# Attention and two feed-forward layers on one core: in batch 0, the value product with unscaled probabilities as stationary operand

## The chip, the cores and the metric

One core of one Trainium2 chip runs the whole program. The metric is the device time of one execution in microseconds. A profiled execution of the same kernel gives the trace from which the rows below come.

## The reference

Causal attention by blocks of 64 over 4 batches, 8 heads, 576 tokens, head size 64; its output, with the heads side by side, is a matrix x of 2304 tokens by 512. Two feed-forward layers follow, each 512 to 2048 to 512, with different nonlinearities. All data is float32.

```python
scores = scale * np.matmul(q, k.transpose(0, 1, 3, 2))
mask = block_i >= block_j                       # blocks of 64 tokens
scores = np.where(mask, scores, -1000000000.0)
scores = scores - np.max(scores, axis=-1, keepdims=True)
attn = np.exp(scores)
attn = attn / (np.sum(attn, axis=-1, keepdims=True) + 1e-09)
attn_out = np.matmul(attn, v)
x = attn_out.transpose(0, 2, 1, 3).reshape(B * S, H * D)
h = x @ w_in;   x = np.maximum(0.01 * h, h) @ w_out            # layer 1
h = x @ w_in2;  g = np.where(h >= 1, h, np.where(h <= -1, 0, (h + 1) ** 2 / 4));  out = g @ w_out2
```

## The kernel before, in words

The kernel keeps float32 accuracy. Most products are made from operands split into a high and a low part of a faster format (three products each, `three`). Only batch 0's attention uses plain float32 products, which the engine runs as two passes, each with its own weight load; `plain_s` and `plain_v` say so for scores and values (`PF` and `VF` are 8 for batch 0, 0 for the others).

A head's 576 tokens are five query tiles (64, then four of 128), in two groups: tiles 0 to 2 (320 tokens) and tiles 3 and 4 (256 tokens). Key chunk 0 has 64 keys, the others 128. For each tile, `scores` (L261) multiplies q by k into a bank of the tag "att" (five banks), VectorE takes the maximum (L286), ScalarE the exponential (L300) and with it the row's sum (the read of the accumulator, same line); VectorE then adds a small constant to the sum and takes the reciprocal (L306 or L308, L309), and GpSimd multiplies the probabilities by it (L47 through `scale`, by `norm_0`). `transposes` (L360) turns each tile by TensorE (L374, two banks of the tag "y"), and ScalarE copies it into the tiles `pT0h` and `pT1h`, keys on partitions. `values` (L403) multiplies, for each group and key chunk, the values as stationary operand (128 columns, of which the first 64 are this chunk's) with all of the group's probabilities as moving operand (128 to 320 columns, L424), into the one bank of the tag "h"; ScalarE copies the first 64 rows of the result into x, which has features on partitions (L432).

While this runs, the weights of layer 1 are loaded and converted: `to_float32` (L104) puts two words together on VectorE (L113 to L115) and scales one on ScalarE or GpSimd by turns (`fE_e`), `split_w` makes high and low parts. After batch 0's attention the blocks of 256 tokens go through layer 1: `split_x` splits x, `up1` (L537 to L539) and `down1` (L567 to L570) multiply, and the attention of batches 1 to 3 is spread between them. `up1` takes the same single "h" bank. Layer 2 comes last.

The program's text is not the order on the engines: `arrange` (L817) runs a model of the engines over all that was traced up to the end of the attention. Each engine takes the ready instruction that stands earliest in the program, with times from `span` (L764), and the order that comes out is written into the program as a chain on each engine, the DMA queue of SyncE included.

## Time and profile before

| | us |
|---|---|
| median of 3 runs | 1029.13 (1028.93 to 1029.42) |
| the profiled execution | 1026.92 |
| its span, first to last instruction | 1025.1 |
| TensorE busy in it | 995.7 (97%) |
| VectorE, ScalarE, GpSimd busy | 709.0, 473.1, 195.8 |

Busy times are sums over the span. An instruction counts as busy from its start to its end, and consecutive ones overlap, so a high share alone does not show that an engine is the one that the others wait for.

### The profile page before, as it was taken

To read this page: it belongs to the slowest core of one execution; us is meant where nothing else is said; L and a number is where in the kernel's file an instruction comes from. 1 tells how busy PE (TensorE), PEld (TensorE's weight loads), DVE (VectorE), ACT (ScalarE), POOL (GpSimd) and SP (SyncE) were. 2 spreads that over 40 slices of the span, in tenths; PEclk is the share of its full clock that TensorE was granted. 3 is DMA by queue.
4 is the path that set the end of the run, shared out by engine and by line. 5 is a ranking of instruction groups with operands and counts; after the bars stand their busy time and mean duration, and the time that the engine had idled before them with its cause. 6 is when DMAs were issued, how large, how long until landed. Compare 5 with 4: busy or idle time off the path is not lost. (4 is left out here: it accounts for less than half of the span.)

```text
span 1025.1 us, 16641 instructions
## 1 busy us (share of the span) xinstructions
PE 995.7 (97%) x5518; PEld 844.8 (82%) x5518; DVE 709.0 (69%) x1859; ACT 473.1 (46%) x1174; POOL 195.8 (19%) x275
## 2 busy tenths in 40 slices
PE   9999999999999999899999999999999999999998
PEld 6668878878878888798989898888888888888897
DVE  7999999997888977887787887334334433443344
ACT  6887767764655545454444443223222222322233
POOL 4452033342242654543010100000000000000000
PEclk9999999999999999999999999999999999999999
DMA  8546232237677766665899784001000100000010
GB/s 320 189 161 224 84 87 61 71 74 160 142 158 154 170 148 145 144 144 107 295 290 297 232 287 104 1 1 61 22 1 1 62 1 1 31 11 0 1 42 20
DMA packets 194117, 115.39 MB, mean 113 GB/s; under 512 B 148208, under 2 KB 167152, under 8 KB 194032
## 3 DMA queue, kind: packets, MB, share of 16 engines
q1 hardware_dynamic: 165840, 106.47, 37.9%
q10 hardware_dynamic: 28192, 7.87, 3.2%
q8 instruction: 43, 0.70, 0.3%
q14 instruction: 42, 0.34, 0.1%
HBM read 83.62 MB, written 30.67 MB: 111 GB/s over the span
## 5 line engine op out<-in xcount | busy, mean ns | idle before, releaser
L537 PE MATMUL h<-xh,w1i 128*128 128x256 f32 x576 | 166.4, 289 | 7.1 <-ACT g L542 6.9
L538 PE MATMUL h<-xl,w1i 128*128 128x256 f32 x576 | 163.7, 285 | 1.0 <-DVE xl L38 0.9
L539 PE MATMUL h<-xh,w1i 128*128 128x256 f32 x576 | 163.4, 284 | 0.0
L719 ACT ACTIVATE sq<-cl,half 128x512 f32<-128x512 f32 (+1 forms) x80 | 54.4, 680 | 200.1 <-DVE cl L718 195.8
L718 DVE TENSOR_SCALAR cl<-hh 128x512 f32<-128x512 f32 (+1 forms) x80 | 51.0, 637 | 111.5 <-PE hh L539 111.3
L537 PEld LDWEIGHTS h<-xh,w1i 128*128 128x128 f32 x576 | 109.1, 189 | 16.8 <-ACT g L542 12.0
L300 ACT ACTIVATE p<-s,nm 64x64 f32<-64x64 f32 (+2 forms) x192 | 91.1, 478 | 63.8 <-DVE nm L286 29.9
L537 PE MATMUL hh<-yh,w2i 128*128 128x512 f32 (+1 forms) x320 | 118.1, 369 | 0.0
L538 PE MATMUL hh<-yl,w2i 128*128 128x512 f32 (+1 forms) x320 | 118.0, 369 | 0.0
L567 PE MATMUL y<-w1o,gh 128*128 128x512 f32 x288 | 117.3, 407 | 0.7 <-DVE yx L575 0.5
L539 PE MATMUL hh<-yh,w2i 128*128 128x512 f32 (+1 forms) x320 | 117.9, 368 | 0.0
L568 PE MATMUL y<-w1o,gh 128*128 128x512 f32 x288 | 114.5, 398 | 0.0
L735 PE MATMUL o<-w2o,ggh 128*128 128x512 f32 x288 | 114.0, 396 | 0.0
L734 PE MATMUL o<-w2o,ggl 128*128 128x512 f32 x288 | 114.0, 396 | 0.0
L538 PEld LDWEIGHTS h<-xl,w1i 128*128 128x128 f32 x576 | 109.0, 189 | 5.5 <-DVE xl L38 1.9
L539 PEld LDWEIGHTS h<-xh,w1i 128*128 128x128 f32 x576 | 109.0, 189 | 0.9
L570 PE MATMUL y<-w1o,gl 128*128 128x512 f32 x288 | 92.4, 399 | 2.7 <-DVE gl L38 2.6
L286 DVE TENSOR_REDUCE nm<-s 128x1 f32<-128x288 f32 (+2 forms) x192 | 80.0, 424 | 8.2 <-PE s L277 4.5
L733 PE MATMUL o<-w2o,ggh 128*128 128x512 f32 x288 | 84.1, 396 | 0.0
L720 DVE TENSOR_TENSOR gg<-hh,sq 128x512 f32<-128x512 f32 (+1 forms) x80 | 50.9, 637 | 47.1 <-ACT sq L719 46.9
L722 DVE TENSOR_TENSOR ggl<-gg,ggh 128x512 fp32r<-128x512 f32 (+1 forms) x80 | 51.1, 638 | 46.7 <-ACT ggh L721 46.2
L542 ACT ACTIVATE g<-h 128x256 f32<-128x256 f32 x144 | 54.2, 378 | 57.5 <-PE h L539 43.1
(111 smaller groups left out, 2038.5 us busy)
## 6 DMA issues: line engine op xcount, KB each, us to landing
wr<-in_w_dram SPq DMA_DIRECT2D x64, 512.0 KB, 5.2
wdram<-wt SPq DMA_DIRECT2D x32, 256.0 KB, 3.9
w<-wdram SPq DMA_DIRECT2D x16, 512.0 KB, 5.6
rq<-in_qkv_dram SPq DMA_DIRECT2D x24, 288.0 KB, 3.0
rk<-in_qkv_dram SPq DMA_DIRECT2D x24, 288.0 KB, 2.9
pT1l<-z SPq DMA_DIRECT2D x16, 384.0 KB, 3.8
ydram<-yx SPq DMA_DIRECT2D x72, 64.0 KB, 2.3
out_dram<-osb ACTq DMA_DIRECT2D x18, 256.0 KB, 3.6
```

The source lines that it names most:

```text
L286: mark["D"] = nc.vector.tensor_reduce(nm[:n, j:j + 1], s[:n, :kw], axis=AX.X, op=ALU.max, negate=True)
L300: mark["A"] = nc.scalar.activation(o, s, AF.Exp, bias=nm[:n, 0:1], scale=es, accum_out=sm[:n, j:j + 1])
L537: nc.tensor.matmul(ps_ap, wh, xh, start=first, stop=False)
L538: nc.tensor.matmul(ps_ap, wh, xl, start=False, stop=False)
L539: nc.tensor.matmul(ps_ap, wl, xh, start=False, stop=last)
L567: nc.tensor.matmul(yt[m], gh[:, ms], wh, start=f == 0, stop=False)
L568: nc.tensor.matmul(yt[m], gh[:, ms], wl, start=False, stop=False)
L570: nc.tensor.matmul(yt[m], gl[:, ms], wh, start=False, stop=f == KF - 1)
L719: nc.scalar.activation(sq[:, :n], cl[:, :n], AF.Square, bias=half[:, 0:1], scale=0.5)
L733: nc.tensor.matmul(ot[m], gh[:, ms], wh, start=f == 0, stop=False)
L734: nc.tensor.matmul(ot[m], gl[:, ms], wh, start=False, stop=False)
L735: nc.tensor.matmul(ot[m], gh[:, ms], wl, start=False, stop=f == KF - 1)
```

## The change

In batch 0 the exponentials are no longer divided by their sum before the transposes. The value product is turned round: for each query tile and key chunk the tile's 128 columns of (unscaled) probabilities are stationary, and the chunk's 64 values with a column of ones are the moving operand (65 columns), so that the result has tokens on partitions and the sum in column 64. One bank holds all five tiles of a head. After the second group VectorE adds the constant to the five sums, takes their reciprocals, and multiplies the 320 results by them into a tile `xt` that a pair of heads shares (it takes the buffers of `pT0l` and `pT1l` by turns). After the odd head TensorE transposes the five tiles of `xt` into two "y" banks, and ScalarE copies these into x. The sum on ScalarE (`accum_out`) goes. The value load writes pieces of 64 elements with gaps between, and the memset of the column of ones is on GpSimd. The conversion's scale is on ScalarE alone (`fE_e`). A branch for unscaled q is added and switched off (`qU` is 'n'). The planner's `span` gets other times for plain float32 products and reciprocals. Batches 1 to 3 keep their code.

```diff
-C = {..., 'fE_e': 'AP', ...}
+C = {'qU': 'n', 'qlE': 'D', ..., 'fE_e': 'A', ..., 'xeE_0': 'A'}
...
         if plain_v(i):
-            nc.sync.dma_start(f32(vv).rearrange("p k a d -> p (k a d)")[:, :vn * D], qkv[row, :, QKC:QKC + vn * D])
-            nc.vector.memset(f32(vv).rearrange("p k a d -> p (k a d)")[:, vn * D:(vn + 1) * D], 0.0)
+            nc.sync.dma_start(f32(vv)[:, :vn, 0], qkv[row, :, QKC:QKC + vn * D].rearrange("p (k d) -> p k d", d=D))
+            nc.gpsimd.memset(f32(vv)[:, :vn, 1, 0:1], 1.0)
...
             mark["A"] = nc.scalar.activation(
-                o, s, AF.Exp, bias=nm[:n, 0:1], scale=es, accum_out=sm[:n, j:j + 1]
+                o, s, AF.Exp, bias=nm[:n, 0:1], scale=es, accum_out=None if plain_v(i) else sm[:n, j:j + 1]
             )
         yield
+        if plain_v(i):
+            return
...
+        if plain_v(i):
+            if g == 0:
+                av[i] = psum(tag, f"v{i}")
+            a = av[i][:, :NKT * (D + 1)].rearrange("p (t d) -> p t d", d=D + 1)
+            hi = ptT(i, g)[0]
+            for t in ts:
+                for c in range(t + 1):
+                    k = 64 if c == 0 else P
+                    q = col(g, c, TILES[t][0] - g0)
+                    nc.tensor.matmul(
+                        a[:, t], hi[:k, q:q + P], f32(vv)[:k, c].rearrange("p a d -> p (a d)")[:, :D + 1],
+                        start=c == 0, stop=c == t,
+                    )
+            yield
+            if g == 1:
+                rc = st_p.tile([P, NKT], F32, tag="rv", name=f"rv{i}", bufs=2)
+                nc.vector.tensor_scalar(rc, a[:, :, D], EPS, None, op0=ALU.add)
+                nc.vector.reciprocal(rc, rc)
+                if h % 2 == 0:
+                    z = h // 2 % 2
+                    xt[b, h // 2] = f32(p_p.tile([P, DW[z]], F32R, tag=f"pT{z}l", name=f"xt{b}_{h // 2}"))[:, :NKT * P].rearrange("p (t c) -> p t c", c=P)
+                x = xt[b, h // 2]
+                d = x[:, :, h % 2 * D:h % 2 * D + D]
+                nc.vector.tensor_tensor(d, a[:, :, :D], rc.unsqueeze(2).to_broadcast([P, NKT, D]), op=ALU.mult)
+                if h % 2 == 1:
+                    yield
+                    for u in range(len(GROUPS)):
+                        u0, un, uts = GROUPS[u]
+                        e = psum(C["T0"], f"xT{i}_{u}")
+                        for t in uts:
+                            q0, n = TILES[t]
+                            nc.tensor.transpose(e[:, q0 - u0:q0 - u0 + n], x[:n, t], ident[:n, :n])
+                        copy(nc, pick("xeE", u, phase(i)), x32[b][:, h // 2, u0:u0 + un], e[:, :un])
+            return
...
-            if plain_v(i):
-                k = 64 if c == 0 else P
-                vr = f32(vv).rearrange("p k a d -> p (k a d)")[:k, c * D:(c + 2) * D]
-                nc.tensor.matmul(a[:, first:gn], vr, ptT(i, g)[0][:k, cs], start=c == 0, stop=c == last)
-                continue
...
-        if plain_v(i):
-            copy(nc, pick("xeE", g, phase(i)), xo, a[:D, :gn])
...
         if srcs[0][3] == F32 and not ins.is_transpose:
-            return w / 0.6 + 165, w / 0.6 + 95, 0
+            step = 2 * max(w / 1.2 + 3, 108) * (1.33 if srcs[1][2][0][1] == 64 and w > 64 else 1)
+            return step + 120, step, 0
...
         if op == "Reciprocal":
-            return 150, 72, 0
+            return 149 + w / 0.96, 71 + w / 0.96, 0
```

## Rows read from the trace of the kernel before

**Rows 1.** Batch 0's stretch: start:end, length, busy PE, PEld, DVE, ACT, POOL; clock; DMA.
```profile
4.60:84.00 79.40, 74.92 (x365) 51.96 (x365) 76.21 (x301) 63.82 (x200) 40.48 (x54) 0.98 0.64 219
```
**Rows 2.** Waits of TensorE, 4 to 85 us: total us, times, longest.
```profile
PE t L374 <- ACT pT1h L30: 2.0, 2, 1.5
PE s L277 <- ACT p L300: 1.6, 2, 1.2
PE t L374 <- issue: 0.7, 1, 0.7
...
```
**Rows 3.** Waits of TensorE, 85 to 200 us.
```profile
PE v L427 <- DVE pT1l L38: 1.1, 1, 1.1
...
```
**Rows 4.** Timeline of the weight loads, 43.5 to 47.9 us: start, us, what, rows*columns.
```profile
44.59 0.19 PEld L277 LDWEIGHTS s<-kh,qs 128*64 128x64 f32 x2 [0.38 <-DVE rc L309]
44.86 0.29 PEld L424 LDWEIGHTS v<-pT1h,vv 64*128 64x128 f32 x2
45.48 1.59 PEld L424 LDWEIGHTS v<-pT1h,vv 128*128 128x128 f32 x8 [0.33 <-issue]
46.99 0.80 PEld L374 LDWEIGHTS t<-ident,p 128*128 128x128 f32 x7
...
```
**Rows 5.** Weight loads by form, 0 to 83 us: busy us, mean ns | idle before.
```profile
L424 PEld LDWEIGHTS v<-pT0h,vv 64*128 64x128 f32 x16 | 2.4, 185 | 3.3 <-ACT pT1h L30 1.3 <-issue 0.9 <-ACT w1o L30 0.7
L277 PEld LDWEIGHTS s<-kh,qs 128*64 128x64 f32 x16 | 1.6, 144 | 1.7 <-issue 0.8 <-DVE rc L309 0.4 <-DVE rc L306 0.2
...
```
**Rows 6.** Timeline of the matmuls around two value products.
```profile
44.86 2.41 PE L424 MATMUL v<-pT1h,vv 64*128 64x256 f32 x10
47.10 0.93 PE L374 MATMUL t<-ident,p 128*128 128x128 f32 x7
...
75.64 1.65 PE L424 MATMUL v<-pT0h,vv 64*128 64x320 f32 x6
77.13 0.71 PE L374 MATMUL t<-ident,p 128*128 128x128 f32 x5
```
**Rows 7.** VectorE's groups of instructions, 0 to 83 us.
```profile
L113 DVE TENSOR_SCALAR wr<-wr 128x512 int32<-128x512 uint32 x16 | 8.1, 508 | 0.0
L309 DVE RECIPROCAL rc<-rc 128x1 f32<-128x1 f32 (+1 forms) x44 | 6.4, 149 | 0.1
L308 DVE TENSOR_SCALAR rc<-sm 128x1 f32<-128x1 f32 (+1 forms) x36 | 4.8, 138 | 0.2 <-ACT p L300 0.2
L38 DVE TENSOR_TENSOR xl<-x,xh 128x256 fp32r<-128x256 f32 x1 | 0.4, 403 | 0.0
...
```
**Rows 8.** The conversion step on VectorE, 83 to 200 us.
```profile
L113 DVE TENSOR_SCALAR wr<-wr 128x512 int32<-128x512 uint32 x16 | 6.5, 431 | 0.0
...
```
**Rows 9.** GpSimd's groups, 0 to 83 us.
```profile
L47 POOL TENSOR_SCALAR p<-p,rc 64x64 f32<-64x64 f32 (+4 forms) x40 | 28.8, 725 | 34.5 <-DVE rc L309 9.7 <-DVE rc L308 8.6 <-ACT pT0h L30 3.3
...
```
**Rows 10.** ScalarE's groups, 0 to 83 us.
```profile
L300 ACT ACTIVATION_READ_ACCUMULATOR p<-s,nm 128x1 f32 (+1 forms) x52 | 10.3, 198 | 0.0
L43 ACT ACTIVATE w<-wr 128x512 f32<-128x512 f32 x10 | 6.7, 674 | 0.0
L30 ACT ACTIVATE x<-v 64x320 f32<-64x320 f32 (+1 forms) x15 | 6.0, 402 | 0.4 <-PE v L424 0.2
...
```
**Rows 11.** Timeline of the end of batch 0's attention, some instructions.
```profile
79.70 3.39 PE L424 MATMUL v<-pT1h,vv 64*128 64x256 f32 x10
80.67 0.72 POOL L38 TENSOR_TENSOR xl<-x,xh 128x256 fp32r<-128x256 f32 x1 [1.18 <-ACT xh L30]
83.13 0.38 ACT L30 ACTIVATE x<-v 64x256 f32<-64x256 f32 x1 [2.02 <-PE v L424]
84.04 0.48 PE L537 MATMUL h<-xh,w1i 128*128 128x256 f32 x1
...
```
**Rows 12.** Two stretches there; columns as in rows 1, the clock after POOL's.
```profile
77.50:80.90 3.40, 1.88 (x12) 1.27 (x10) 3.36 (x15) 3.32 (x10) 1.11 (x2) 1.00 0.22 80
80.90:84.30 3.40, 3.40 (x15) 3.03 (x14) 3.12 (x9) 1.33 (x5) 1.52 (x3) 0.50 0.71 223
...
```

More of the change, by code (lines that the diff above doesn't have):

```diff
@@ L212, in attention_moe_moe @@
     stk = {}
+    av, xt = {}, {}
     def plain_s(i):
@@ L217, in plain_s, with unscaled @@
         return p < len(C["PF"]) and h < C["PF"][p]
+    def unscaled(i):
+        return pick("qU", 0, phase(i)) == "y"
     def plain_v(i):
@@ L241, in load_head @@
             nc.sync.dma_start(r, qkv[row, :, q0:q1])
-            scale(nc, pick("qhE", 0, ph), qs[:, q0:q1], r, SCALE)
-            nc.vector.scalar_tensor_tensor(
-                out=qs[D:, q0:q1], in0=r[D:], scalar=SCALE, in1=f32(qs)[D:, q0:q1], op0=ALU.mult, op1=ALU.subtract
-            )
+            if unscaled(i):
+                copy(nc, pick("qhE", 0, ph), qs[:, q0:q1], r)
+                tt(nc, pick("qlE", 0, ph), qs[D:, q0:q1], r[D:], f32(qs)[D:, q0:q1], ALU.subtract)
+            else:
+                scale(nc, pick("qhE", 0, ph), qs[:, q0:q1], r, SCALE)
+                nc.vector.scalar_tensor_tensor(
+                    out=qs[D:, q0:q1], in0=r[D:], scalar=SCALE, in1=f32(qs)[D:, q0:q1], op0=ALU.mult, op1=ALU.subtract
+                )
             r = raw_p.tile([P, S], F32, tag="raw", name=f"rk{i}")[:, :kn]
@@ L268, in scores @@
         nm = st_p.tile([P, 2], F32, tag="nm", name=f"nm{i}_{t}")
-        sm = st_p.tile([P, 2], F32, tag="sm", name=f"sm{i}_{t}")
-        rc = st_p.tile([P, 1], F32, tag="rc", name=f"rc{i}_{t}")
+        if not plain_v(i):
+            sm = st_p.tile([P, 2], F32, tag="sm", name=f"sm{i}_{t}")
+            rc = st_p.tile([P, 1], F32, tag="rc", name=f"rc{i}_{t}")
         sc = []
@@ L292, in scores @@
             sc.append((p[:n].rearrange("p (a k) -> p a k", a=2), halves))
-        es = SCALE / 2 if plain_s(i) else 1.0
+        es = SCALE / 2 if plain_s(i) else SCALE if unscaled(i) else 1.0
         if np_ > 1:
@@ L407, in values @@
         g0, gn, ts = GROUPS[g]
+        if h == 0 and g == 0:
+            x32[b] = one_p.tile([P, KC, S], F32, tag="x", name=f"x{b}", bufs=2)
+        if plain_v(i):
[10 more added lines that the diff above has]
+                        start=c == 0, stop=c == t,
+                    )
+            yield
[19 more added lines that the diff above has]
+            return
         a = psum(tag, f"v{i}_{g}")
         last = ts[-1]
-        if h == 0 and g == 0:
-            x32[b] = one_p.tile([P, KC, S], F32, tag="x", name=f"x{b}", bufs=2)
         own, other = (0, D) if h % 2 == 0 else (D, 0)
@@ L430, in values @@
                 )
[L431 to L440 removed]
+        tmp = two_p.tile([P, 320], F32, tag="sc", name=f"tmp{i}_{g}", bufs=C["sc"])
+        nc.scalar.activation(tmp[own:own + D, :gn], a[other:other + D, :gn], AF.Copy)
+        if pick("fold", 0, phase(i)) == "D":
+            nc.vector.tensor_tensor(xo, a[own:own + D, :gn], tmp[own:own + D, :gn], op=ALU.add)
+        else:
+            nc.scalar.activation(xo, a[own:own + D, :gn], AF.Copy)
+            nc.gpsimd.tensor_tensor(xo, xo, tmp[own:own + D, :gn], op=ALU.add)
         yield
```

9 lines of the change are left out of this document (1 added, 8 removed).

## The prediction

> **What bounds the kernel now.** I read the busy time by stretch first. While batch 0's attention runs, up to the first matrix product of the feed-forward part at 84 us, TensorE is busy 74.92 of 79.40 us and VectorE 76.21 [rows 1]. Both look full, so the question is which one makes the other wait. TensorE's own list of waits settles it: between 4 and 85 us it stands still for 4.5 us in all (four rows, the three longest shown), and 1.5 of these are one wait, at 79.6 us [rows 2]. From 85 to 200 us its waits come to 2.9 us (five rows, the first shown) [rows 3]. VectorE fills its gaps with the conversion of weights that the next stage wants. So TensorE paces batch 0 and most of what follows: what the change adds on TensorE is paid nearly in full, and what it takes from the other engines brings back at most those waits.
>
> A busy TensorE also has gaps inside. The weight loads of the value product show them: two loads of 64 rows go back to back (0.29 us for two), then the loads of 128 rows start only after 0.33 us of idle [rows 4]. The first stream starts when the first load is done, at 44.97 us; two streams of 256 columns at 0.213 us end at 45.39, and the next load starts at 45.48, so 0.09 us after the stream. With equal rows the loads hide behind streams: eight loads take 1.59 us, one per stream. I count a change of rows (64 to 128 or back) as 0.09 us of idle plus a load of 0.107 us that is not hidden.
>
> **The change part by part: TensorE.** Before, a head's value product runs from 44.86 to 47.10 us for the second group (2.24 us) and from 75.64 to 77.13 for the first (1.49) [rows 6]; with 0.09 us ahead of each for the change into 64 rows that is 3.91 us, with 4 changes of rows in it.
>
> After, a head has 15 products (1+2+3+4+5 key chunks), each in two passes as now: 30 passes. The stationary operand is the 128 columns of probabilities and only 65 columns stream (0.054 us), so the load sets the pace. Two loads of this width take 0.29 us together and one alone 0.185, so they follow each other by some 0.107; and that a load hides behind a stream as short as this is seen at 44.59 us, where two loads of 64 columns take 0.19 us together and one alone 0.144, the second one starting 0.05 us after the first, as the first stream starts [rows 4, 5]. With the start of the stream I count 0.108 us a pass. 30 x 0.108 = 3.24 us. Key chunk 0 has 64 rows and now comes once per query tile, not once per group: going into it and out of it makes 8 changes of rows per head (tiles 0 and 1 share one stretch) in place of 4. At a change, one pass costs 0.054 + 0.09 + 0.107 = 0.25 us, 0.145 more than 0.108: 8 x 0.145 = 1.16. The load behind each group is half uncovered, 0.05 us twice. Sum 4.50 us against 3.91: +0.59 per head, +4.7 us for eight.
>
> New are the transposes of x, five per pair of heads: 5 x 0.11 (seven transposes' loads take 0.80 us [rows 4]) and the 64-token tile's two changes of rows, 2 x 0.15, makes 0.85 us, or 3.4 us for four pairs. TensorE gets 4.7 + 3.4 = 8.1 us more work. Bounds: if the added changes of rows cost nothing, 4 x 0.145 x 8 = 4.6 us go, and 3.5 are left; if nothing hides behind 65 columns, each pass costs 0.161 (30 x 0.161 + 8 x 0.09 = 5.55 per head) and the sum is over 16 us. The pair of 64-column loads speaks against that end, so I take 8.1, and for the range the case that no wait is recovered.
>
> A rule of the Trainium skill (TensorE: Matmul & The Clock Gate, section "Part 3: Packing small matmuls", on what overlaps) says that weight loads overlap a running matmul only where their row group differs. The rows above show the reverse here: equal rows overlap, a change of rows leaves 0.33 us. By the rule the added changes would be free, and TensorE's part of the sum about 3.5 us.
>
> **The other engines.** VectorE loses 40 additions (0.138 us) and 40 reciprocals (0.149 us) [rows 7], 11.5 us busy, though consecutive small ones overlap by about half, so 8 us; eight memsets go to GpSimd. It gains per head an addition, a reciprocal and a product of 320 elements: 0.14 + 0.15 + 0.50 (0.403 for 256 elements [rows 7], in proportion) = 0.79, or 6 us. GpSimd loses the 40 normalisations, 28.8 us [rows 9]; one of the steps that convert weights on VectorE takes 0.508 us in this stage, with them about [rows 7]; a later one without such company, 0.431 [rows 8], so 16 x 0.08 = 1.2 us come back there, perhaps twice that with the other steps. In all VectorE gets 3 to 5 us lighter. ScalarE loses 48 accumulator reads (0.198) and 16 copies of x (0.402), gains 8 wider copies of about the same length and six conversions (0.674) from GpSimd [rows 10]: 9.5 + 6.4 - 3.2 - 4.0, so 9 us lighter. None of this is on the path; its worth is that TensorE's transposes no longer wait for sum, reciprocal and normalisation, which is part of the 4.5 us in [rows 2]. Without the wait at the end of the stage 3.0 us are to be had; ScalarE's copies and the score banks still stand behind some of it, so I take 2.5, between 0 and 3.0. In the following stage conversion is further ahead; of the 2.9 us I take 1.5, between 0 and 2.9. The value load now lands in five pieces of 256 B per partition; it is issued a head ahead, and I cost it at nothing, as its cover is a whole head (some 9 us). The disabled branch (unscaled q) and the planner's new estimates do no work on the chip; the latter give other orders, for which I allow 1.5 us either way.
>
> **The handover.** Now the last head's second group ends, ScalarE copies x out of the one "h" bank (at 83.13 us), and the feed-forward starts at 84.04 [rows 11]. After, the bank is free only when VectorE's three operations are done, and the last quarter of x goes through them (0.79), transposes (0.9), a copy (0.4), the split on ScalarE and GpSimd (0.4 + 0.72 [rows 11]): with hand-offs about 4 us, of which three quarters of the first product (9 of 12 passes, 84.04 to 85.1) and batch 1's scores and transposes cover most. The batch 1 tiles pT0l and pT1l now wait for the transposes of x, which takes away some of that cover. Against this the present stall of 1.5 us [rows 2] and the half clock behind it should go or be replaced by the same. Net +0.5 us, between -2.5 and +2.
>
> Sum: 8.1 - 2.5 - 1.5 + 0.5 = +4.6 us on the profiled execution's 1026.92, so 1031.5; the median of the runs shown is 2.2 us above that execution, which gives **1033.7 us**.
>
> **The rivals.** First, no change: the weight loads of 64 and of 128 rows overlap in the new order, so the added changes of rows cost nothing, TensorE's addition is 3.5 us, and the recovered waits pay for it: 3.5 - 2.5 - 1.5 + 0.5 = 0, 1029.1 us. For it: the planner may put chunk 0 of neighbouring tiles next to the 64-token transposes. Against: the change of rows in [rows 4] has its idle. The rule of the skill named above would have it so. Chance 0.17.
>
> Second, faster: VectorE paces the stage after all; its 76.21 of 79.40 us [rows 1] leaves no room, and what is taken from it, up to 5 us, carries through to the end of conversion. TensorE's 8.1 us then fall into gaps between its instructions that the list of waits does not show, and 4.5 us remain as gain: 1024.6 us. It decides if those gaps are over 8 us in the stage; against it, all waits listed come to 4.5 us [rows 2]. Chance 0.17.
>
> Third, slower by more: the clock. It was at half in one stretch, 80.9 to 84.3 us, right after TensorE was busy only 1.88 of 3.40 us [rows 12]; there ten value passes took 3.39 us against 2.41 [rows 6, 11], so a fall costs 1 to 1.7 us. The changed kernel streams 30 x 0.054 = 1.6 us per head in the value product, where now 2 x 1856 columns (320 + 128 + 128 and five times 256) stream for 3.1. If gaps there bring three more falls, +4.2 us: 1038 us. Chance 0.16.
>
> **How the numbers follow.** The forecast has 0.50, with 1030.5 to 1037.5 as its own range. A measurement of this kernel tells about 0.2% (2 us) from no change. Faster: 0.17 from the second rival and 0.02 from the first; same: 0.13 from the first and 0.05 from the forecast; the rest is slower, 0.63. The range leaves out most of the second rival and reaches over the third: 1026.5 to 1039.5, which takes in the case in which no wait comes back (8.1 + 2, 1039.2).
>
> **What would show it.** Right: the first feed-forward product starts 4 to 7 us later than 84.04; the loads of the new value product have a pace near 0.108 us with idle "issue" of about 0.2 us before each change of rows; GpSimd nearly empty; TensorE's waits in this stage no more than before. Wrong: loads of 64 and 128 rows without idle between them, a first product at or before 84 us, VectorE no longer full, or several stretches at half clock before 85 us.

## The result and the profile after

The changed kernel takes 1040.1 us (median of 4 runs, 1038.4 to 1045.2) against 1029.0 for the kernel before in the same series: 1.0121 times as long, interval 1.0101 to 1.014. It is slower, as forecast, but by 11.1 us where 4.6 were forecast, and above the upper end of the range. The profiled execution is one of the four, 1040.94 us with a span of 1039.2: 14.0 us above the profiled execution of before. Some 3 of these 14 us belong to the two executions and not to the kernels: the one profiled after lies 0.8 us above its kernel's median, the one before 2.1 below.

The page's first part for the changed kernel (busy us, share of the span, number of instructions):

```profile
PE 1006.9 (97%) x5650; PEld 861.5 (83%) x5650; DVE 709.6 (68%) x1795; ACT 470.9 (45%) x1124; POOL 161.8 (16%) x237
```

TensorE has 11.2 us more, GpSimd 34 us less, and VectorE is where it was over the whole span. Where the 14 us arose is read from three points of TensorE's timeline: the last matmul of batch 0's value products, the first matmul for the fourth column of 128 hidden features in the first block's `up1`, and the last matmul of all (the start of each). I call the stretch up to the first point the body and that between the first and the second the end; three columns of `up1` lie in it.

| us | body ends | end ends | length of the end | rest, to the last matmul |
|---|---|---|---|---|
| before | 82.7 | 92.1 | 9.4 | 928.8 |
| after | 86.7 | 106.1 | 19.4 | 928.9 |
| difference | +4.0 | | +10.0 | +0.1 |

The forecast had +5.6 for the body (8.1 of work less 2.5 of waits), +0.5 for the end and -1.5 for the rest.

The view of stretches, of the changed kernel: start:end, length, busy time of PE, PEld, DVE, ACT and POOL, granted clock, DMA share, GB/s. The first row is the body, the second the end, the other four show how the end goes:

```profile
4.60:86.70 82.10, 80.92 (x487) 63.33 (x486) 73.15 (x236) 61.92 (x150) 4.90 (x12) 0.98 0.66 217
86.70:106.10 19.40, 14.69 (x72) 12.96 (x71) 16.05 (x43) 11.27 (x28) 5.17 (x4) 0.74 0.63 220
86.70:89.30 2.60, 0.71 (x9) 0.57 (x7) 2.54 (x11) 1.56 (x3) 1.85 (x2) 0.98 0.47 134
89.30:92.70 3.40, 3.40 (x15) 3.06 (x16) 3.31 (x10) 1.76 (x7) 0.00 (x0) 0.52 0.82 227
92.70:96.00 3.30, 0.95 (x9) 0.73 (x8) 2.54 (x6) 2.93 (x8) 2.65 (x1) 1.00 0.97 364
96.00:102.80 6.80, 6.33 (x23) 5.65 (x24) 5.15 (x12) 3.56 (x9) 0.67 (x1) 0.50 0.51 210
```

The same view of the kernel before, for the same two stretches (the stretch in [rows 1] goes on to 84.0):

```profile
4.60:82.70 78.10, 73.62 (x358) 50.66 (x358) 75.12 (x298) 62.99 (x197) 39.66 (x53) 0.99 0.63 217
82.70:92.10 9.40, 9.40 (x63) 8.77 (x63) 9.09 (x25) 8.54 (x22) 4.23 (x3) 0.92 0.82 269
```

In the body TensorE has 7.3 us more to do and 3.3 us less to wait for, which gives the 4.0. In the end it was never idle before; now it is idle for 4.7 of 19.4 us, and the clock is 0.74 on average, so 2 x (1 - 0.74) x 19.4 = 10.1 of the 19.4 us run at 1.2 GHz, the lower of the two levels of the clock.

The timeline of the end in the changed kernel, some instructions (start, us, engine, line, operation, idle time before it and what released it):

```profile
87.12 0.28 PE L291 MATMUL s<-kl,qs 128*64 128x64 f32 x1
...
88.65 0.49 DVE L444 TENSOR_TENSOR xt<-v,rv 128x320 f32<-128x320 f32 x1
89.06 0.20 DVE L305 TENSOR_SCALAR nm<-nm 128x1 f32<-128x1 f32 x1
...
89.29 0.55 PE L574 MATMUL h<-xh,w1i 128*128 128x256 f32 x1 [1.89 <-DVE nm L305]
...
91.05 1.41 PE L452 MATMUL xT<-ident,xt 64*128 64x64 f32 x5
92.07 0.81 ACT L30 ACTIVATE x<-xT 128x320 f32<-128x320 f32 x2 [1.64 <-PE xT L452]
92.78 0.41 ACT L30 ACTIVATE xh<-x 128x256 fp32r<-128x256 f32 x1
93.24 0.38 PE L574 MATMUL h<-xh,w1i 128*128 128x256 f32 x1
93.27 2.65 POOL L38 TENSOR_TENSOR xl<-x,xh 128x256 fp32r<-128x256 f32 x1 [4.30 <-ACT xh L30]
95.97 0.58 PE L575 MATMUL h<-xl,w1i 128*128 128x256 f32 x1 [2.35 <-POOL xl L38]
```

The last head's result lies in the only "h" bank until VectorE's product (L444) has read it at 89.14 us. `up1` wants this bank, and TensorE stands still from 87.40 to 89.29. The releaser named, nm L305, is the instruction that VectorE issued next; what ended the wait by the names of the tiles is L444, the last reader of the bank (TensorE starts 0.15 us after its end, here and at the same place of three other kernels). Its time is short; it is late because VectorE's queue has a conversion step, another tile's maximum and a subtraction in front and in between. Then `up1` starts at half the clock. The transposes of x (L452) stand in the middle of its order, the copy and the split follow, and GpSimd's subtraction `xl`, which took 0.72 us before [rows 11], takes 2.65 us here (the last section shows why); TensorE waits 2.35 us for it. The clock, full again from 92.7 us while TensorE is nearly idle, falls once more at 96.0, for 6.8 us. Before, one copy on ScalarE, 0.38 us, stood between the value product and `up1` [rows 11].

### The profile page after: what moved, and what is told of

It is laid out like the page before. It is cut to its first block, busy times and chain, and to the rows that moved or that the text cites. A ratio compares the mean times of both kernels' runs of the same rounds, so it can differ in the third digit from the quotient of the medians.

```text
span 1039.2 us, 16671 instructions
## 1 busy us (share of the span) xinstructions
PE 1006.9 (97%) x5650; PEld 861.5 (83%) x5650; DVE 709.6 (68%) x1795; ACT 470.9 (45%) x1124; POOL 161.8 (16%) x237
## 5 line engine op out<-in xcount | busy, mean ns | idle before, releaser
L574 PE MATMUL h<-xh,w1i 128*128 128x256 f32 x576 | 168.2, 293 | 8.9 <-ACT g L579 6.8
L575 PE MATMUL h<-xl,w1i 128*128 128x256 f32 x576 | 165.8, 288 | 3.5 <-POOL xl L38 2.5
L576 PE MATMUL h<-xh,w1i 128*128 128x256 f32 x576 | 165.4, 288 | 0.0
L574 PEld LDWEIGHTS h<-xh,w1i 128*128 128x128 f32 x576 | 110.6, 192 | 18.4 <-ACT g L579 11.6
L309 ACT ACTIVATE p<-s,nm 128x288 f32<-128x288 f32 (+2 forms) x192 | 89.8, 478 | 63.6 <-DVE nm L295 28.9
L576 PEld LDWEIGHTS h<-xh,w1i 128*128 128x128 f32 x576 | 110.9, 193 | 0.7
L295 DVE TENSOR_REDUCE nm<-s 128x1 f32<-128x288 f32 (+2 forms) x192 | 79.5, 422 | 10.1 <-PE s L286 5.4
```

The costliest lines, as they stand in the source:

```text
L295: mark["D"] = nc.vector.tensor_reduce(nm[:n, j:j + 1], s[:n, :kw], axis=AX.X, op=ALU.max, negate=True)
L309: mark["A"] = nc.scalar.activation(o, s, AF.Exp, bias=nm[:n, 0:1], scale=es, accum_out=None if plain_v(i) else sm[:n, j:j + 1])
L574: nc.tensor.matmul(ps_ap, wh, xh, start=first, stop=False)
L575: nc.tensor.matmul(ps_ap, wh, xl, start=False, stop=False)
L576: nc.tensor.matmul(ps_ap, wl, xh, start=False, stop=last)
```

## The experiments

Times are medians; "body" and "end" are the two points and the length defined above, from the profiled execution of each kernel. The ratios compare with the kernel before within one series; it took 1027.3 to 1029.0 us in the several series. The theory after the first result: TensorE's added work is as forecast, and the lost 10 us lie in the end, where the new chain (bank, division, transposes, copy, split) makes idle time and idle time brings the half clock. The rivals: the changes of rows cost it, the clock costs it by itself, or the planner's new estimates do.

### The last two heads the old way

Heads 6 and 7 of batch 0 keep the old value product, sums and normalisation; the other six are turned round.

```diff
+    def turned(i):
+        return plain_v(i) and heads[i][1] < 6
...
-        if plain_v(i):
+        if turned(i):
```

> The changed kernel, but heads 6 and 7 of batch 0 keep the value product and the normalisation of the kernel before; heads 0 to 5 are as changed. Theory of the end: most of the loss beyond the forecast comes after the last value product, because the last pair's result must pass VectorE, TensorE's transposes, a copy and the split before the feed-forward can go on. Then this kernel saves 7 to 9 us there and about 2 us of TensorE's work in two heads: 1029 to 1032 us. Theory of the body: the loss is spread evenly over the heads, a quarter of it goes: about 1037 us. Theory of the planner: another order of the later stages makes the loss, and this changes little in a predictable way: 1036 to 1042 us.

Measured: 1035.8 us, ratio 1.0072 (1.0046 to 1.0097). The end shrinks from 19.4 to 9.7 us, the length that it had before; TensorE is idle in it for 0.27 us and the clock is full (the view of stretches, this kernel):

```profile
90.40:100.10 9.70, 9.43 (x69) 8.35 (x67) 9.55 (x28) 8.62 (x22) 3.93 (x4) 1.00 0.70 230
```

So the chain behind the last pair makes the whole loss of the end, its half clock included. The body did not come back with it: it ends at 90.4, with two falls of the clock in it (from 47.6 and 68.0 us), and so only some 4 us of the kernel's 11 were regained: the theory of the end had expected 1029 to 1032 us. Of the 3.7 us by which this body is longer, 2.3 are more waits of TensorE (3.5 us in all, 1.2 in the changed kernel).

### Fewer changes of rows

Key chunk 0 gets 128 rows for all tiles but the first (the added 64 rows of values and ones are zero; the value load becomes two transfers, with two more small memsets on GpSimd), so that 40 changes of rows are left in the body, where the changed kernel has 82 and the kernel before 44.

```diff
+            nc.gpsimd.memset(f32(vv)[64:, 0].rearrange("p a d -> p (a d)")[:, :D + 1], 0.0)
...
-                    k = 64 if c == 0 else P
+                    k = 64 if t == 0 else P
```

> The changed kernel, but key chunk 0 is multiplied with 128 rows from query tile 1 on (its upper 64 rows of values are zeros; the value load is two transfers and a memset). The changes of rows in the value product fall from 8 to 2 per head, the passes stay 30. If a change of rows costs 0.145 us each, as in the prediction, TensorE's work falls by 6 x 0.145 x 8 = 7 us and the first feed-forward product starts 5 to 7 us earlier than at 89.3; the time is about 1034 us. If changes of rows cost nothing (the rival), no difference: 1040 us. What happens after the last value product is as in the changed kernel in both theories.

Measured: 1029.4 us, ratio 1.0005 (0.999 to 1.002). The body ends at 82.7, 4.0 us earlier than after and level with before. Its waits rose in turn (TensorE's list of waits, this kernel, 4 to 86 us: total, times, longest):

```profile
PE v L433 <- DVE xt L447: 2.4, 2, 1.6
PE t L388 <- ACT pT1h L30: 0.8, 1, 0.8
```

Against 1.2 us of waits in all in the changed kernel's body this is 2.2 us more, so the 42 changes taken away are worth 6.2 us of TensorE's time, about 0.15 us each (it is busy there for 74.73 us, 80.92 in the changed kernel, with 3.4 us at half clock in both), and 4.0 of these arrive. One group of 16 loads shows the same by itself: in the changed kernel it has one stretch of 64 rows inside, so two changes, and takes 0.29 us longer than here, where it has none (timeline of the weight loads, first the changed kernel, then this one):

```profile
84.66 2.15 PEld L430 LDWEIGHTS v<-vv,pT1h 128*128 128x128 f32 x16
80.95 1.86 PEld L433 LDWEIGHTS v<-vv,pT1h 128*128 128x128 f32 x16
```

The time was expected at 1034 us, with nothing changed after the last value product; but there, too, it became shorter, by more than in the body. The end is 15.4 us, 4.0 shorter, with the clock at 0.89 in place of 0.74: one fall of 3.4 us in place of 3.4 and 6.8, and GpSimd's subtraction takes 0.73 us here. The rest is 5 us shorter too (923.7). This edit explains neither; the experiments on orders below show differences of that size.

### The last pair group by group, and matmuls to fill the end

One kernel divides, transposes and copies the last two heads group by group, each group in a bank of its own. The other issues ten matmuls of 256 columns whose results nobody reads, five behind the last value product and five behind the first copy of x, to take the idle time away and leave the chain.

```diff
-            if g == 0:
-                av[i] = psum(tag, f"v{i}")
+            each = h >= 6
+            if g == 0 or each:
+                av[i] = psum(tag, f"v{i}_{g}")
...
```

> The changed kernel, but for heads 6 and 7 the two groups have a bank each and are normalised, and for head 7 transposed and copied, as soon as each group's product is done; all products stay as changed, with a few more small VectorE operations. Theory of the end: the first block's 256 tokens are ready before the second group's product, the wait for the split (2.4 us) and the half clock behind it (about 5 us) go: 1031 to 1034 us, with no half clock between 89 and 103 us. Theory of the body or of the planner: within 2 us of the changed kernel, about 1040 us.

```diff
+            if h == 7 and g == 1:
+                fill_a = psum("att", "fill_a")
+                for _ in range(5):
+                    nc.tensor.matmul(fill_a[:, :256], ident, hi[:, :256], start=True, stop=True)
...
```

> The changed kernel with ten more float32 products of 256 columns whose result is not used (about 0.43 us each at the full clock): five right behind the last value product, five behind the copy of x for the first block, where TensorE stands still 1.9 and 2.4 us in the changed kernel. Theory of the clock: the half clock from 89 to 92.6 and from 96 to 102.8 us costs about 5 us; the filler takes time in which TensorE waits anyway and keeps the clock up, so 1035 to 1037 us and at most one stretch at half clock there. If the clock costs little and the loss is the waiting itself, or if the filler delays the work: 1040 to 1044 us.

Measured: by group 1037.3 us, 1.0094 (1.0065 to 1.0124), end 12.3 us; the body is longer, 91.2, with a fall from 47.0 us that lasts 6.8 us, where the changed kernel had 3.4, and a second one from 87.9 that reaches far into the end:

```profile
87.90:98.20 10.30, 9.54 (x45) 8.48 (x44) 7.23 (x22) 5.55 (x16) 3.12 (x4) 0.50 0.72 231
```

So the expectation that the half clock between 89 and 103 us goes is not met, although the wait for the split is gone and TensorE is idle for only 0.8 us of the end; a wait of 1.8 us for VectorE's queue, before the second group's product, now stands ahead of the fall. With the filler 1040.6 us, 1.0136 (1.0105 to 1.0168), end 14.5 us:

```profile
87.20:101.70 14.50, 13.93 (x87) 12.15 (x86) 14.46 (x33) 8.14 (x18) 7.34 (x4) 1.00 0.78 268
```

Ten products of two streams at some 0.213 us are 4.3 us of filler, and 0.57 us of idle are left: together about the 4.7 us that TensorE idled there in the changed kernel. With the idle time filled the clock stays full, and the end is 4.9 us shorter. That is the clock's part of the end, and in this execution it went with the idle time: without the filler's 4.3 us TensorE is busy for 9.6 us here, for 14.7 in the changed kernel, where 10.2 ran at half clock. The kernel as a whole gained nothing (1035 to 1037 us had been expected): its body has two falls (from 47.6 and 68.1 us), and its rest took 931.8 us, 2.9 more than that of the changed kernel.

### The pieces of the end: the bank, and GpSimd's subtraction

The value product of batch 0 takes its bank from the five of the scores, so that `up1` has the "h" bank for itself:

```diff
-'V0': 'h'
+'V0': 'att'
```

> The changed kernel, but batch 0's value products use the score banks and not the bank that the first feed-forward product needs. If the 1.9 us in which that product waits for VectorE's normalisation, and the stretch at half clock that follows, are what costs, the feed-forward starts before the normalisation is done: the stretch from the last value product to the fourth column is 14 to 16 us, the time 1035 to 1037 us. If only the last quarter of x counts, the wait moves behind it: 18 to 20 us, 1040 us. The score banks lose one to the products, which may cost some us in the heads.

The subtraction `xl` of the last quarter of x goes from GpSimd to VectorE:

```diff
-'xlE_0': 'PDPP'
+'xlE_0': 'PDPD'
```

> The changed kernel, but the low part of the last quarter of x (and of that quarter alone) for the first block is subtracted on VectorE and not on GpSimd, where it took 2.65 us beside VectorE's conversions. If this subtraction is what holds the end up, the wait of 2.35 us goes, and with it the second, longer stretch at half clock (96 to 102.8 us, worth 3.4 us): the stretch from the last value product to the fourth feed-forward column is 14 us instead of 19.4 and the time 1034 to 1036 us. If the chain ahead of it (bank, transposes, copy) is late anyway: 18 to 19 us and 1038 to 1040 us.

Measured: own bank 1033.8 us, 1.005 (1.003 to 1.007), the largest gain among the kernels that keep 64 rows in chunk 0: `up1` starts at 67.6 us already, with the quarters of x that are there, the body ends at 83.2 and the end takes 16.2. TensorE's waits from 80 to 110 us in it:

```profile
PE s L290 <- DVE nm L295: 1.9, 1, 1.9
PE h L575 <- POOL xl L38: 1.2, 1, 1.2
PE h L574 <- ACT xh L30: 0.9, 1, 0.9
```

`up1` no longer waits for the bank, but what stands behind it waits for the same queue of VectorE, and the clock falls once, for 6.8 us from 89.2. With `xl` on VectorE 1037.5 us, 1.0077 (1.0053 to 1.0101): the wait for `xl` is gone (its subtraction took 0.43 us), the wait for the bank is the same 1.9 us, and the end is 16.2 us at a clock of 0.68. The half clock did not go with the wait for `xl`: one fall of 10.2 us from 96.7 stands where the changed kernel has 3.4 and 6.8. And with the bank of its own TensorE is still idle for 4.3 us of the end, where the changed kernel has 4.7; its 16.2 us also hold less work, as a part of `up1`'s first column lies in the body. So each piece gives back a few microseconds, and none gives back the 10.

### The clock in the body

To lengthen what streams, 100 columns move in place of 65 (the others are ones that nobody reads):

```diff
-            a = av[i][:, :NKT * (D + 1)].rearrange("p (t d) -> p t d", d=D + 1)
+            a = av[i][:, :NKT * 100].rearrange("p (t d) -> p t d", d=100)
...
```

> The changed kernel, but 100 columns stream where 65 did (35 more columns of ones, whose results nobody reads); the order on every engine is the same. The weight load of 128 columns (0.108 us) still covers a stream of 100 columns (0.083 us), so the passes keep their pace and only the changes of rows get longer, by 8 x 0.03 us per head, 1.9 us in all. Theory of the clock: TensorE drops to half speed in batch 0's attention because the turned product streams so little; with half as much again streamed, the time at half clock falls from about 25 us (mean of the timed runs) to 10 to 15, which is worth 4 to 7 us: 1035 to 1038 us. Without that effect: 1042 us, with as much time at half clock.

Measured: 1040.8 us, 1.0123 (1.0094 to 1.0152), the same as the changed kernel. The order on every engine is the changed kernel's own. The view of stretches for the bodies of this kernel and of the one with `xl` on VectorE, whose TensorE order is the changed kernel's through all of batch 0, and below them the longest fall of the latter:

```profile
4.60:86.50 81.90, 80.76 (x486) 61.93 (x486) 73.51 (x236) 61.92 (x150) 6.00 (x12) 1.00 0.66 218
```
```profile
4.60:94.40 89.80, 89.05 (x487) 68.99 (x486) 73.14 (x236) 61.92 (x150) 5.01 (x12) 0.87 0.60 199
69.40:83.10 13.70, 13.70 (x47) 10.09 (x47) 6.71 (x22) 4.72 (x12) 1.44 (x3) 0.50 0.29 89
```

With 100 columns the body of this execution has no fall and ends at 86.5; in the changed kernel 3.4 us of it were at half clock, which costs at most 1.7 us, and the wider stream costs about as much. On TensorE the second kernel runs the same instructions in the same order as the changed kernel up to there, and its body is 7.7 us longer, with 23.9 us at half clock. The falls of the body thus differ from one execution to the next. That fits the timed runs: from the mean granted clock c, the time at half clock is 2(1 - c) of the span, which is 21, 17, 25 and 38 us in the four runs of the changed kernel, the longest of them in the slowest run (1045.2 us), and about 9.5 us in those of the kernel before. On the mean that is 25 us against 9.5, and half of the difference, nearly 8 of the 11 us, is the clock's; this is an estimate from granted clocks, and where in these runs the falls lie is not recorded. The four runs of the wide kernel have 21, 15, 23 and 25 us, so the wider stream did not bring the 10 to 15 us that the theory of the clock named. With the last pair the old way, or with 128 rows, it is 14 us on the mean, by group 26. The end of the wide kernel is unchanged, 19.1 us, with falls at the same two places (88.7 and 95.6).

The falls are of two kinds. In the stretch of 3.4 us just before each fall at the end of batch 0 TensorE was busy for 0.8 to 2.0 us, in all kernels that have one. Before the fall at 48.2 us in the body of the changed kernel it was busy all the time, at the full clock:

```profile
44.80:48.20 3.40, 3.40 (x23) 2.83 (x24) 3.20 (x8) 2.65 (x8) 0.00 (x0) 1.00 0.91 281
```

Eight more falls of this second kind lie in the bodies of other kernels (last pair the old way, by group, filler, old estimates, `xl` on VectorE). All nine are in kernels with 65 columns and 64 rows in chunk 0; none is in the profiled executions with 100 columns, with 128 rows, or with the old product. Idle time does not explain these. Whether the short streams do, as the third rival has it, is not shown: the timed runs with 100 columns do not bear it out.

### The planner's estimates

The changed kernel with the old times in `span`, and the kernel before with the new ones:

```diff
-            step = 2 * max(w / 1.2 + 3, 108) * (1.33 if srcs[1][2][0][1] == 64 and w > 64 else 1)
-            return step + 120, step, 0
+            return w / 0.6 + 165, w / 0.6 + 95, 0
...
```

> The changed kernel with the planner's old estimates for plain float32 products and reciprocals (65 columns: 203 ns where the new ones give 216 or 287); the work is the same, only the order on the engines may differ. Theory of the work (TensorE's added passes, changes of rows and the chain at the end make the loss): the last value product stays at 86 to 88 us, the loss after it stays, 1037 to 1043 us. Theory of the planner (the new estimates brought a worse order): most of the 11 us goes, below 1034 us.

> The kernel before with the changed kernel's estimates and nothing else of the change. It shows how far another order alone moves the time: 1.5 us either way was allowed for in the prediction, so 1027 to 1031 us. If the later stages answer to any new order by several us, as the runs so far suggest (the distance to the kernel before changes by up to 5 us after 110 us), 1024 to 1035 us with the same first 80 us.

Measured: the changed kernel with the old estimates 1038.6 us, 1.0091 (1.0073 to 1.0109), end 15.6 us. Its body ends at 90.9 and not at 86 to 88: a fall from 65.2 us lasts 13.7 us, and the execution profiled (1043.7 us) is one of its slower ones. So the theory of the planner, below 1034 us, is not borne out, and the 1.5 us to the changed kernel lie within the scatter of the runs. The kernel before with the new ones 1033.7 us, 1.0053 (1.0032 to 1.0074): it loses 4.7 us although no instruction is added or taken away, and although its first 80 us are better. The view of stretches for it:

```profile
4.60:80.00 75.40, 72.62 (x354) 50.19 (x354) 70.48 (x288) 62.20 (x194) 38.01 (x53) 1.00 0.61 208
80.00:130.00 50.00, 45.45 (x284) 38.65 (x283) 49.76 (x111) 33.12 (x74) 3.94 (x5) 1.00 0.50 170
```

and for the kernel before:

```profile
4.60:80.00 75.40, 70.92 (x350) 48.66 (x349) 72.48 (x292) 61.89 (x194) 38.94 (x52) 1.00 0.64 222
80.00:130.00 50.00, 49.43 (x308) 43.87 (x307) 49.49 (x111) 34.16 (x79) 5.82 (x5) 0.97 0.44 149
```

TensorE issues 4 matmuls more in the first stretch, and 24 fewer in the second, with VectorE full. It waits there 3.7 us for the nonlinearity (ACT g), in the kernel before 0.5. VectorE has 19 conversions of weights (L115) in that stretch, 17 in the kernel before, and ScalarE waits for them for 11.2 us, in the kernel before 6.2. So an order that is better up to the handover can leave VectorE behind after it.

### What the removed work is worth, and 128 rows in the old product

The kernel before without sums, reciprocals and normalisation in batch 0 (it leaves out the division there, nothing else):

```diff
-                o, s, AF.Exp, bias=nm[:n, 0:1], scale=es, accum_out=sm[:n, j:j + 1]
+                o, s, AF.Exp, bias=nm[:n, 0:1], scale=es, accum_out=None if plain_v(i) else sm[:n, j:j + 1]
...
+        if plain_v(i):
+            return
```

> The kernel before without batch 0's sums, reciprocals and normalisation: the row sums on ScalarE, the additions and reciprocals on VectorE and the multiplication on GpSimd are left out, so batch 0's probabilities are not divided by their sum. This is the gain that the change could have at most from what it takes away. The prediction's terms: 2.5 us from waits in batch 0 and 1.5 us later, so 1025 us. VectorE as the pacer (second rival): all of its 8 us show, 1021 us or less. If these waits are replaced by others: 1028 to 1029 us.

The kernel before with 128 rows in key chunk 0 of its value product (the added rows of values and probabilities are zero; the value load is two transfers, and the zeros are two more memsets per head on VectorE):

```diff
+                nc.vector.memset(pT[k][0][64:, :64], 0.0)
...
+            nc.vector.memset(vf[64:, :D], 0.0)
...
-                k = 64 if c == 0 else P
+                k = P
```

> The kernel before, with key chunk 0 of the plain value product multiplied with 128 rows (upper 64 rows of values zero; the value load is two transfers and one more memset): 4 changes of rows per head fall away, streams and passes stay. If each costs 0.09 us of idle and 0.107 us of uncovered load, 32 x 0.2 = 6.3 us of TensorE's work go, and with TensorE as the pacer the last value product comes 4 to 6 us before 82.7 and the time is 1023 to 1026 us. If changes of rows cost nothing, or VectorE paces the stage: 1028 to 1030 us.

Measured: without the division 1026.6 us, 0.9981 (0.9964 to 0.9999). That is 2.4 us, all that this removal brings if nothing is added for it. In the profiled execution the body ends at 80.3, so 2.4 us earlier, the end is 0.8 longer and the rest 1.5 shorter. TensorE is idle for 1.7 us of this body, where the kernel before has 4.5, and there is no fall of the clock before 400 us. With 128 rows 1031.3 us, 1.0025 (1.0008 to 1.0042), which is slower, although 26 of the 44 changes of rows in the body are gone (18 are left; the 64-token transposes keep theirs): the body ends at 88.3, with a fall of the clock from 82.0 that lasts 6.8 us, and TensorE waits in it for copies and probabilities (4 to 85 us, the first rows):

```profile
PE t L379 <- ACT pT1h L30: 3.0, 5, 0.7
PE t L379 <- POOL p L47: 2.5, 3, 1.8
PE s L282 <- ACT p L305: 1.1, 4, 0.4
```

The stretch of this body reads:

```profile
4.60:88.30 83.70, 74.61 (x365) 54.26 (x365) 79.42 (x311) 66.48 (x205) 40.47 (x53) 0.96 0.64 211
```

TensorE is idle for 9.1 us of it, 4.6 more than before. Of its busy time 6.3 us are at half clock, so at the full clock it would be some 71.5 us, against 72.7 before: its own work, with seven matmuls more, fell by little more than 1 us, where 6.3 had been expected. So here the changes of rows were not worth what they are in the changed kernel, and the waits for the engines that feed TensorE grew by more than it gained. Whether the added memsets on VectorE, another order, or TensorE's lead over these engines made them, the rows do not tell.

### Versions that put the pieces together

All have 128 rows in key chunk 0 from tile 1 on, by the edit shown above (heads 6 and 7 the old way keep their 64), and one or two of the other edits shown: the last pair group by group; the last pair the old way; 100 columns; an own bank and `xl` on VectorE.

> Both repairs together: key chunk 0 with 128 rows from query tile 1 on, and the last pair normalised, transposed and copied group by group. If the two act on different places (the changes of rows in all heads; the chain after the last product), their gains add: 1029.4 less 2 to 4 us, 1025 to 1028 us, and the stretch from the last value product to the fourth block column of the feed-forward (15.4 us with the first repair alone, 9.4 in the kernel before) is near 12. If it was the order of later stages that made the first repair look good: 1030 to 1036 us.

> Key chunk 0 with 128 rows in heads 0 to 5, and heads 6 and 7 with the value product and normalisation of the kernel before. The end costs what it does in the kernel before (last value product to fourth feed-forward column 9 to 10 us); the body saves 6 x 0.145 x 6 = 5 us of changes of rows against the kernel that only keeps the last pair (1035.8): 1029 to 1032 us. If the changes of rows cost nothing, 1036 us.

> Key chunk 0 with 128 rows from tile 1 on, and 100 columns streamed instead of 65. With two changes of rows per head left, the wider stream costs 0.5 us in all. Theory of the clock: time at half clock from 14 us (128 rows alone) to about 10, as in the kernel before: 1027 to 1029 us. Without it: 1030 us.

> 128 rows for key chunk 0 from tile 1 on, the subtraction on VectorE and the products in the score banks. If the three act on different places: the last value product at 82 to 84 us, the end 11 to 12 us, and 1025 to 1028 us, at or below the kernel before. If the end needs the chain whatever its parts: 15 us, 1029 to 1031 us.

| | us | ratio, interval | body ends | end |
|---|---|---|---|---|
| 128 rows, by group | 1028.2 | 1.0008 (0.999 to 1.0025) | 88.5 | 12.8 |
| 128 rows, last pair the old way | 1027.8 | 1.001 (0.9994 to 1.0027) | 84.9 | 9.8 |
| 128 rows, 100 columns | 1031.0 | 1.0035 (1.0018 to 1.0051) | 81.5 | 15.6 |
| 128 rows, own bank, `xl` on VectorE | 1029.8 | 1.0016 (1.0001 to 1.0031) | 79.5 | 16.1 |

None that computes everything is faster than the kernel before; 128 rows alone and three of these four are within 0.2% of it. The gain of the 42 changes of rows and that of a shorter end do not add up: 128 rows alone stands at 1.0005, and each further piece leaves it there or above. The points in the table are those of one execution each: by group it was the slowest of ten, with 12.4 us of its body at half clock. With the own bank `up1` starts at 63.8 us already, so its end holds less work.

## Why the prediction was wrong, point by point

**The body was forecast right.** The first feed-forward product starts at 89.29 us, 5.3 later than before, within the 4 to 7 us named. GpSimd is nearly empty (4.90 us busy in the body, 39.66 before). The product of 320 elements on VectorE takes 0.484 us (0.50 forecast), the conversion step 435 ns where it took 508 [rows 7] and 431 was forecast [rows 8]. VectorE's groups in the changed kernel, 0 to 83 us and 0 to 90 us (mean ns behind the busy time):

```profile
L113 DVE TENSOR_SCALAR wr<-wr 128x512 int32<-128x512 uint32 x18 | 7.7, 435 | 0.0
```
```profile
L444 DVE TENSOR_TENSOR xt<-v,rv 128x320 f32<-128x320 f32 x8 | 3.9, 484 | 0.0
```

TensorE's busy time in the body rose by 7.3 us where 8.1 were forecast, its idle time fell from 4.5 to 1.2 us, by 3.3 where 2.5 were forecast. (Some 0.8 of the 7.3 are the clock's, with 3.4 us of the body at half in place of 1.8, and one of the four pairs' transposes lies in the end: 6.5 us of work at the full clock, where the terms give 7.3 without that pair.) The twelve passes of a head's first group show the pace (timeline of the weight loads, changed kernel; the view joins loads of 64 and of 128 rows of one line):

```profile
63.63 1.84 PEld L430 LDWEIGHTS v<-vv,pT0h 64*128 64x128 f32 x12 [0.30 <-issue]
```

With 0.185 for the last load, eleven steps of 0.108 and three changes of rows of 0.145 the forecast's terms give 1.81 us for these; 1.84 were taken. Over the whole body, outside the fall of the clock, loads of the value product with equal rows start 0.110 us after each other (median of 171), at a change of rows 0.255 (37 of them): the forecast had 0.108 and 0.25.

**The failed step is the handover**, a term mis-sized: +0.5 us, between -2.5 and +2, against +10.0 measured. These 9.5 us are the miss of the profiled execution (1040.9 against 1031.5): the body's -1.6 and the rest's +1.6 against their terms cancel. The chain in it was named (bank, three operations on VectorE, transposes, copy, split), but it was taken as covered by three quarters of the first product and batch 1's work. Three things were missed. The bank that the chain holds is the one that the cover itself needs, so the cover could not start: 1.9 us. The three operations were counted at their own 0.79 us and not with what VectorE's queue puts before and between them; and the subtraction on GpSimd was counted at 0.72, where it took 2.65 and TensorE waited 2.35 us for it. With a third wait of 0.5 that makes 4.7 us of idle time. Then the clock: 10.2 us at half in this stretch, where before had 1.5 (its fall from 80.9 reaches to 84.3 [rows 12], and 82.7 is where the stretch begins), costs about half of the difference, 4.3 us. The remaining 1.0 us is more work in the stretch (72 matmuls, 63 before). The run with the old last pair shows that all of it hangs on the chain, the filler shows the clock's 4.9 us. How long the end becomes with the chain in it depends on what else stands in the queues: with the same chain in other orders it is 15.4 and 15.6 us (128 rows, old estimates), some 6 us more than before and not 10; the wait for the subtraction is 2.35 us in this order, 0.8 with the old estimates, none with 128 rows.

**The third rival, the clock, came true together with this step**, in another place than forecast: in the profiled execution not the short streams of the value product gave most of it, but the idle time of the end (10.2 of some 21 us at half clock, where before had 10 in all and 1.5 there). Its time, 1038 us, was the nearest of the four. The handover of the kernel before had already shown such a fall once, behind a stretch with much idle time [rows 12]; I counted that one as going away or staying, not as growing. In the body there is one fall of 3.4 us in the changed kernel, one to three in most others, none in the wide one; which of them an execution gets is not settled by the order. Those that come with TensorE busy are nearest to what this rival had in mind, and it is open what brings them.

**The first rival falls.** Were the changes of rows free, taking 42 of them away would bring nothing; it took 6.2 us off TensorE's busy time and brought 4.0 us in the body. The rule of the Trainium skill that it went by (TensorE: Matmul & The Clock Gate, section "Part 3: Packing small matmuls"), that a load overlaps only where the row group differs, does not describe these loads: equal rows overlap. That 64 and 128 rows would count as groups that differ was this prediction's own step.

**The second rival falls**: TensorE waits for other engines in the body for 1.2 us only, and VectorE, no longer full, is busy for 73.15 of its 82.10 us, so TensorE paces it. In the kernel before, too, taking VectorE's work away brought 2.4 us and not 8.

**The recovered waits.** The 2.5 us of the body are borne out twice, by the idle time (3.3 us) and by the removal of the division alone (2.4 us). The 1.5 us later are not there in the changed kernel, whose rest took 0.1 us more. The removal alone has 1.5 of them in its rest, but loses 0.8 in its end, and its medians show 2.4 us in all, not 4.

**The allowance for another order**, 1.5 us, was too small: new estimates alone cost the kernel before 4.7 us, and the old ones in the changed kernel give 1.5 us by the medians, which its runs do not set apart from nothing. How much of the 11 us is the order's cannot be separated from the chain in the end, since the order decides what stands before and between the chain's steps.

## What to carry to other kernels

When a change puts a longer chain behind the last product of a stage, follow it through each engine's queue and each bank up to the first instruction of the next stage, and ask whether the work that is to cover it needs a buffer that the chain still holds. Idle time on TensorE was paid about twice at this place, once as idle time (4.7 us) and once as half clock after it (4.3). Where a planner sets the order, run its new estimates alone on the old kernel: here they cost as much as everything that I had forecast.

## What the runs showed of the hardware

A change between weight loads of 64 and of 128 rows costs about 0.15 us in the changed kernel (42 of them, 6 us), while loads of equal rows follow each other every 0.11 us behind streams of only 65 columns. The granted clock fell to half in different places in executions with the same TensorE order: 3.4 us of the body at half in one, none in another with wider streams, 23.9 us in a third.

The length of GpSimd's subtraction has a reason that can be read. VectorE's timeline in the changed kernel while the subtraction runs from 93.27 to 95.92 us:

```profile
93.10 0.11 DVE L293 MEMSET s<- 64x64 f32 x1 [0.49 <-PE s L291]
93.13 0.67 DVE L115 SCALAR_TENSOR_TENSOR w<-w,wr 128x512 int32<-128x512 int32 x1
93.72 0.67 DVE L114 SCALAR_TENSOR_TENSOR wr<-wr 128x512 int32<-128x512 int32 x1
94.32 0.41 DVE L113 TENSOR_SCALAR wr<-wr 128x512 int32<-128x512 uint32 x1
94.65 0.68 DVE L115 SCALAR_TENSOR_TENSOR w<-w,wr 128x512 int32<-128x512 int32 x1
95.69 0.78 DVE L38 TENSOR_TENSOR w1i<-w,w1i 128x512 fp32r<-128x512 f32 x1 [0.36 <-ACT w1i L30]
```

Four conversion steps follow each other without a gap up to 95.33, and the subtraction ends 0.59 us after that. In the wide kernel VectorE's steps end at 94.92 and the subtraction (2.63 us) at 95.50; with the own bank 88.25 and 88.83 (1.53 us); with the old last pair 88.53 and 89.12 (1.05); by group 90.64 and 91.24 (1.14). So it does its work in the 0.6 us after VectorE's last step of this kind, however early it was issued; where nothing is in its way it takes 0.72 (128 rows by group). But a train of steps does not always keep it out: with the filler it came in between two of them, ended 0.58 us after the first, and the second, L114, took 1.21 us where 0.67 is usual (POOL and VectorE, that kernel):

```profile
92.40 0.74 POOL L38 TENSOR_TENSOR xl<-x,xh 128x256 fp32r<-128x256 f32 x1 [2.97 <-ACT xh L30]
91.87 1.82 DVE L114 SCALAR_TENSOR_TENSOR wr<-wr 128x512 int32<-128x512 int32 x2
```

The Trainium skill (SBUF — State Buffer, section "Who interferes with whom") says that a VectorE instruction with two inputs in SBUF and a GpSimd instruction that reads SBUF contend. These timelines agree, and they add that a train of such steps can keep GpSimd out for all of its length (2.65 us), or GpSimd's instruction can hold up a step of the train. The train above also has a step with one input (L113); why that one did not let the subtraction in is not shown. No kernel was made to test this alone; the one with `xl` on VectorE fits it.
